# Three VectorE operations instead of six in a split of fp32 weights, and attention chunks that alternate between two batches

## The chip, the cores and the metric

The kernel runs on one core of a Trainium2 chip. The metric is the device time of one execution in microseconds; before the change it is 609.76 us, the median of three runs from 607.66 to 609.99.

## The reference

A decayed linear attention (2 batches, 8 heads, 768 positions, head size 64) feeds two feed-forward blocks in fp32 (512 to 2048 to 512 columns, 1536 tokens), the first with ELU, the second with softplus:

```python
for b in range(nb):                      # blocks of 64 positions
    intra = np.einsum('bhic,bhjc->bhij', qb, kb) * Dmask[None]
    intra = np.einsum('bhij,bhjd->bhid', intra, vb)
    inter = np.einsum('bhid,bhde->bhie', qb * lam_pow[None], kv_state)
    out[:, :, sl] = intra + inter
    kv_state = lam_block[None, :, None, None] * kv_state + np.einsum('bhsd,bhse->bhde', kb_dec, vb)
...
h = x @ w_in;  g = where(h > 0, h, exp(min(h, 0)) - 1);  x = g @ w_out
h = x @ w_in2; g = maximum(h, 0) + log1p(exp(-abs(h)));  y = g @ w_out2
```

## The kernel before

Attention works in chunks of 128 positions, six per batch, twelve in all, `g` counting through batch 0 and then batch 1. A chunk has three slots of TensorE work: "s" (`att_s`, scores, then masked by VectorE at L234), "t" (`att_state`, the new state from keys that ScalarE has scaled at L212, summed by VectorE at L281 and multiplied by the decay on POOL at L285, `faded`) and "x" (`att_x`, the output from scores and from the state of the chunk before, split into `xh` by ScalarE at L263 and `xl` by VectorE at L264). POOL multiplies the queries by decay powers at L206. The loads of later chunks (`qk`, `kv`) are issued in `att_next` from SP, after a chunk's "x".

The feed-forward weights come as float64, 16 blocks of 1 MB for each layer (`raw`), and `split_w` makes two fp32r parts of each: `wh`, and the remainder `wl`. It is a generator that is advanced piece by piece by `w_ops`. A piece is one VectorE operation, with what ScalarE does beside it; there are six: L99 and L101 assemble the low bits of the word, L106 and L109 rebuild the fp32 value in `t`, L112 keeps its exponent, L120 makes `wl`. ScalarE does L98 (a scaled copy of the high words) and L119 (`wh`). The last piece issues the load of the next block but one (`load_w`, L75); `raw` has two buffers.

Each product is three fp32r matmuls (`wh` with `xh`, `wh` with `xl`, `wl` with `xh`), 128 x 512 wide. There are 96 steps, 48 for each layer, two of them lagging: step n issues `m1(n)` (12 wide matmuls, L350 to L352), the activation, and `m2(n-2)` (12 wide matmuls, L415). Before step 0, 13 of attention's 36 slots are run, which completes the four chunks of the first token tile; steps 0 to 7 take three slots each. Steps 0 to 3 have 8 dummy matmuls each (`warm(4)` is traced as 8) and advance the split by 8 pieces, later steps by 4; eight splits are wanted by step 8, and from step 13 on `w_start` starts one every two steps, in three groups of eight, the second group's end and the third in layer 2 or shortly before it.

TensorE's and SP's orders are as written by hand throughout. Up to step 7 the orders of ScalarE, VectorE and POOL are set by a planner that goes by priorities (attention and the first activations stand above the splits); from step 8 on only VectorE's is. Every engine runs its own list in order.

Of the kernel before, what the change touches and what calls it, by code (L numbers as in the profile page):

```python
# [15 lines left out]
P = 128  # L16
# [20 lines left out]
def body(ctx, tc, lamc, ident, attqk, attkv, w1, w2, out):  # L37
# [31 lines left out]
    def load_w():  # L69
        if wnext[0] == len(wqueue):  # L70
            return
        layer, fc = key = wqueue[wnext[0]]
        wnext[0] += 1
        raw[key] = stage.tile([P, 2 * DM], U64, tag="raw", name="raw")
        nc.sync.dma_start(out=raw[key], in_=weights[layer][fc])  # L75
# [15 lines left out]
    def split_w(key):  # L91

        word = raw.pop(key).bitcast(U32).rearrange("p (n two) -> p n two", two=2)
        low, high = word[:, :, 0], word[:, :, 1]
        r = conv.tile([P, 2 * DM], F32, tag="r", name="r")
        ri = r.bitcast(U32)

        A.activation(out=r, in_=high.bitcast(F32), func=AF.Copy, scale=2.0 ** -112)  # L98
        V.tensor_scalar(out=high, in0=high, scalar1=23, scalar2=None, op0=ALU.logical_shift_left)  # L99
        yield  # L100
        V.scalar_tensor_tensor(  # L101
            out=high, in0=low, scalar=9, in1=high, op0=ALU.logical_shift_right, op1=ALU.bitwise_or)
        yield
        t = conv.tile([P, 2 * DM], F32, tag="t", name="t")
        ti = t.bitcast(U32)
        V.tensor_scalar(  # L106
            out=ti, in0=ri, scalar1=3, scalar2=0x7FFFF000, op0=ALU.logical_shift_left, op1=ALU.bitwise_and)
        yield
        V.scalar_tensor_tensor(  # L109
            out=ti, in0=ri, scalar=0x80000000, in1=ti, op0=ALU.bitwise_and, op1=ALU.bitwise_or)  # L110
        yield
        V.tensor_scalar(out=ri, in0=ti, scalar1=0xFF800000, scalar2=None, op0=ALU.bitwise_and)  # L112
        yield
        fc = key[0] * NF + key[1]
        k = fc % RING
        pool = wp if k < 8 else late["acc"]
        hi = pool.tile([P, 2 * DM], F32R, tag=f"wh{k}", name=f"wh{k}")
        lo = pool.tile([P, 2 * DM], F32R, tag=f"wl{k}", name=f"wl{k}")
        A.activation(out=hi, in_=t, func=AF.Copy)  # L119
        V.scalar_tensor_tensor(out=lo, in0=high, scalar=2.0 ** -43, in1=r, op0=ALU.mult, op1=ALU.mult)  # L120
        load_w()
        for i in range(2):
            o = slice(i * DM, i * DM + DM)
            wh[fc, i], wl[fc, i] = hi[:, o], lo[:, o]
# [76 lines left out]

    def att_prep(g):

        if g % CPB:
            q = at[g][0].rearrange("p (a i) -> p a i", a=NPAIR)
            G.tensor_tensor(out=q, in0=q, in1=qpow, op=ALU.mult)  # L206

    def att_prep_k(g):
        if g < NCHUNK and g % CPB < CPB - 1:
            for h in range(H):  # L210
                k = at[g][2][:, D * h:D * h + D]
                A.activation(out=k, in_=k, func=AF.Copy, scale=kdecay[:, h:h + 1])  # L212
# [26 lines left out]
    def att_x(g):  # L239
        a = at[g]  # L240
        ps = a_psum("xps")
        first = g % CPB == 0

        for p in range(0 if first else NPAIR):
            o = slice(P * p, P * p + P)
            for e in range(2):
                r = slice(64 * e, 64 * e + 64)
                T.matmul(ps[r, o], state[g - 1][r, p, :], a[0][r, o], start=(p == 0), stop=False, skip_group_check=True)  # L248
        for p in range(NPAIR):
            o = slice(P * p, P * p + P)  # L250
            for e in range(2):
                h = 2 * p + e
                T.matmul(  # L253
                    ps[64 * e:64 * e + 64, o], a[3][:, D * h:D * h + D], sc[g][:, e, p, :],
                    start=first, stop=True, skip_group_check=True,
                )
        t, c = divmod(g, TT // P)
        if c == 0:
            new_x(t)
        o = slice(c * P, c * P + P)  # L260
        ps = ps.rearrange("p (a i) -> p a i", a=NPAIR)
        hi, lo = xh[t][:, :, o], xl[t][:, :, o]
        A.activation(out=hi, in_=ps, func=AF.Copy)  # L263
        deferred.append(lambda: V.tensor_tensor(out=lo, in0=ps, in1=hi.bitcast(F32), op=ALU.subtract))  # L264

    def att_state(g):
        if g % CPB == CPB - 1:
            return
        a = at[g]
        ps = a_psum("stps")[:, :NPAIR * D]  # L270
        for p in range(NPAIR):
            for e in range(2):
                r = slice(D * e, D * e + D)
                o = slice(P * p + D * e, P * p + D * e + D)
                T.matmul(ps[r, D * p:D * p + D], a[2][:, o], a[3][:, o], start=True, stop=True, skip_group_check=True)
        ps = ps.rearrange("p (a i) -> p a i", a=NPAIR)
        state[g] = ap2.tile([P, NPAIR, D], F32, tag="state", name="state")
        if g % CPB == 0:
            V.tensor_copy(state[g], ps)
        else:  # L280
            V.tensor_tensor(out=state[g], in0=ps, in1=faded.pop(g - 1), op=ALU.add)  # L281
        if g % CPB < CPB - 2:
            faded[g] = ap2.tile([P, NPAIR, D], F32, tag="faded", name="faded")
            decay = qpow[:, :, P - 1:P].to_broadcast([P, NPAIR, D])
            G.tensor_tensor(out=faded[g], in0=state[g], in1=decay, op=ALU.mult)  # L285

# [116 lines left out]
    def m2(n):  # L403
        u, c = order[n]
        layer, t, begin, end = units[u]
        fc = layer * NF + c
        if c == begin:
            for m in range(KD):
                yps[m] = ps_y.tile([P, TT], F32, tag=f"y{m}", name=f"y{m}")
        g = gt.pop(n)  # L410
        for m in range(KD):
            s = slice(P * m, P * m + P)
            for i, (gi, wt) in enumerate(((0, wh[fc, 1]), (1, wh[fc, 1]), (0, wl[fc, 1]))):
                a, b = (wt[:, s], g[:, gi]) if layer == 0 else (g[:, gi, s], wt)
                T.matmul(yps[m], a, b, start=(c == begin and i == 0), stop=(c == end - 1 and i == 2))  # L415
        if c < end - 1:
            return
        summed = yacc.get((layer, t))
        if end < NF:
            if summed is None:  # L420
                yacc[layer, t] = new_acc(free.pop())
            for m in range(KD):
                if summed is None:
                    A.activation(out=yacc[layer, t][m], in_=yps[m], func=AF.Copy)
                else:
                    V.tensor_tensor(out=summed[m], in0=yps[m], in1=summed[m], op=ALU.add)
        elif layer == 0:
            new_x(t)
            for m in range(KD):
                if summed is None:  # L430
                    hi = xh[t][:, m, :]
                    A.activation(out=hi, in_=yps[m], func=AF.Copy)
                    V.tensor_tensor(out=xl[t][:, m, :], in0=yps[m], in1=hi.bitcast(F32), op=ALU.subtract)
                else:
                    y = summed[m]
                    V.tensor_tensor(out=y, in0=yps[m], in1=y, op=ALU.add)
                    split.append((t, y, m))
        else:
            if summed is None:
                o = xp.tile([P, KD, TT], F32, tag=f"xl{t}", name="o")  # L440
            for m in range(KD):
                r = t * TT + m * P
                if summed is None:
                    y = o[:, m, :]
                    A.activation(out=y, in_=yps[m], func=AF.Copy)
                else:
                    y = summed[m]
                    V.tensor_tensor(out=y, in0=yps[m], in1=y, op=ALU.add)
                nc.sync.dma_start(out=out[r:r + P, :], in_=y)
# [10 lines left out]

    def step(n):
        last = len(order) - 1
        pieces = 4 if n < 4 else 2

        early = n < LAG
        if early:
# [38 lines left out]
    with tc.manual_schedule(engines={ET.SP, ET.PE}):  # L505
        setup()
        decays()
        att_prep_k(0)
        while len(slots) > 3 * (NCHUNK - TT // P) - 1:
            refill()  # L510
            att_slot()
            w_ops(1, True)
        for n in range(8):
            step(n)
    with tc.manual_schedule(engines={ET.PE, ET.Activation, ET.Pool, ET.SP}):
# [7 lines left out]
def _layout(q, k, v, lam, win, wout, win2, wout2):  # L523
    def t(x):

        x = x.reshape(B, NPAIR, 2, CPB, P, D).transpose(0, 3, 2, 5, 1, 4)
        return x.reshape(NCHUNK, P, DM)

    def n(x):

        x = x.reshape(B, H, CPB, P, D).transpose(0, 2, 3, 1, 4)
        return x.reshape(NCHUNK, P, DM)

    def w(a, b):
# [30 lines left out]
```

## Time and profile before

| | |
|---|---|
| median of three runs | 609.76 us |
| lowest, highest | 607.66, 609.99 us |
| span of the profiled execution | 606.8 us |
| busy in the span: TensorE, its weight loads | 584.5, 480.0 us |
| busy: VectorE, ScalarE, POOL | 408.8, 340.7, 174.7 us |
| mean granted clock of TensorE | 0.994 of full |
| read from memory, written | 46.21, 3.15 MB |

The profile holds one execution; the page gives its span, first to last instruction, and no other time for it. Views used are the page (busy times, and the span in 40 slices of 15.2 us with busy shares in tenths), the busy times in chosen stretches, instructions grouped by source line, the list in order of time, the waits, and the chain of work that ended last.

### The profile page before, as it was taken

What the parts mean: (1) busy time and instruction counts of PE and PEld (TensorE: products, weight loads), DVE (VectorE), ACT (ScalarE), POOL (GpSimd) and SP (SyncE); (2) the same over time, 40 slices, a digit from 0 to 9 for tenths busy, and PEclk for the clock granted to TensorE, in tenths of its full rate; (3) what the DMA queues carried; (4) which work ended last, traced back from release to release, by engine and by line L of the source; (5) the groups of instructions that cost most, each with busy time, mean ns of one, the idle gap of its engine ahead of it and who ended that gap; (6) DMA issues with size and microseconds to landing.
All of it is one profiled execution on the core that took longest, in us unless ns stands there. A gap on an engine that the chain in (4) does not pass through costs nothing.

```text
span 606.8 us, 7845 instructions
## 1 busy us (share of the span) xinstructions
PE 584.5 (96%) x3058; PEld 480.0 (79%) x3058; DVE 408.8 (67%) x469; ACT 340.7 (56%) x577; POOL 174.7 (29%) x130
## 2 busy tenths in 40 slices
PE   7887899999999999999999999999999999999997
PEld 6775777888888888888888877887878888888885
DVE  6999973114578672216877996559999995565655
ACT  4756544244564553245555765757877775655552
POOL 1423223022122221253253363123223222222122
PEclk9999899999999999999999999999999999999999
DMA  8853652000322411001213111001213100100101
GB/s 321 343 210 139 252 187 82 1 0 1 119 91 69 139 69 71 0 1 63 77 70 139 69 70 69 1 0 64 77 70 138 70 1 2 69 1 1 70 1 69
DMA packets 10117, 49.86 MB, mean 82 GB/s; under 512 B 1248, under 2 KB 1376, under 8 KB 5984
## 3 DMA queue, kind: packets, MB, share of 16 engines
q1 hardware_dynamic: 10080, 49.36, 22.2%
q8 instruction: 24, 0.39, 0.2%
q14 instruction: 13, 0.11, 0.1%
HBM read 46.21 MB, written 3.15 MB: 81 GB/s over the span
## 4 chain that ended last, share of the span: by engine, by line
PE 80%; DVE 9%; issue 4%; ACT 3%; DMA 2%; POOL 2%; SPq 0%; DVEq 0%; ACTq 0%; POOLq 0%
PE y L415 38%; PE hps L351 13%; PE hps L350 13%; PE hps L352 13%; DMA qk<-attqk 1%; DVE t L109 1%; DVE raw L101 1%; DVE t L106 1%; PE xps L248 1%; PE xps L253 1%; DMA kv<-attkv 1%; PE sps L231 1%; DVE u L379 1%; POOL g L391 1%; DVE l L387 1%
## 5 line engine op out<-in xcount | busy, mean ns | idle before, releaser
L350 PE MATMUL hps<-xh,wh 128*128 128x512 f32 x384 | 151.1, 394 | 1.7 <-ACT xh L263 1.7
L351 PE MATMUL hps<-xl,wh 128*128 128x512 f32 x384 | 150.4, 392 | 2.2 <-DVE xl L264 2.2
L352 PE MATMUL hps<-xh,wl 128*128 128x512 f32 x384 | 150.0, 391 | 0.0
L415 PE MATMUL y<-wh,g 128*128 128x512 f32 x384 | 120.7, 392 | 3.3 <-POOL g L391 3.0
L391 POOL TENSOR_TENSOR g<-l,g 128x512 fp32r<-128x512 f32 x48 | 68.9, 1436 | 185.1 <-ACT g L390 159.6
L391 POOL TENSOR_TENSOR g<-v,g 128x512 fp32r<-128x512 f32 x48 | 65.7, 1368 | 187.0 <-ACT g L390 187.0
L415 PE MATMUL y<-g,wh 128*128 128x512 f32 x384 | 119.0, 391 | 0.0
L361 ACT ACTIVATE v<-hps 128x512 f32<-128x512 f32 x48 | 28.7, 597 | 122.9 <-PE hps L352 122.9
L385 DVE SCALAR_TENSOR_TENSOR v<-v,hps 128x512 f32<-128x512 f32 x48 | 32.8, 684 | 90.1 <-ACT v L362 89.8
L415 PEld LDWEIGHTS y<-wh,g 128*128 128x128 f32 x384 | 72.1, 188 | 21.9 <-POOL g L391 6.6
L351 PEld LDWEIGHTS hps<-xl,wh 128*128 128x128 f32 x384 | 72.5, 189 | 17.7 <-DVE xl L264 2.8
L350 PEld LDWEIGHTS hps<-xh,wh 128*128 128x128 f32 x384 | 72.5, 189 | 17.5 <-ACT xh L263 1.9
L352 PEld LDWEIGHTS hps<-xh,wl 128*128 128x128 f32 x384 | 72.5, 189 | 15.1
L415 PEld LDWEIGHTS y<-g,wh 128*128 128x128 f32 x384 | 71.6, 188 | 15.5 <-issue 0.2
L379 DVE SCALAR_TENSOR_TENSOR u<-u,e 128x512 f32<-128x512 f32 x48 | 44.0, 917 | 56.4 <-ACT l L373 56.4
L415 PE MATMUL y<-wl,g 128*128 128x512 f32 x192 | 74.8, 390 | 0.0
L415 PE MATMUL y<-g,wl 128*128 128x512 f32 x192 | 74.8, 389 | 0.0
L370 ACT ACTIVATE e<-hps 128x512 f32<-128x512 f32 x48 | 28.7, 597 | 68.9 <-PE hps L352 68.9
L387 DVE TENSOR_TENSOR l<-l,u 128x512 f32<-128x512 f32 x48 | 61.7, 1286 | 3.7
L120 DVE SCALAR_TENSOR_TENSOR wl<-raw,r 128x1024 fp32r<-128x1024 uint32 x32 | 46.5, 1453 | 1.0 <-DVE r L112 0.5
L119 ACT ACTIVATE wh<-t 128x1024 fp32r<-128x1024 f32 x32 | 33.8, 1056 | 22.1 <-DVE t L109 21.7
L415 PEld LDWEIGHTS y<-g,wl 128*128 128x128 f32 x192 | 36.0, 188 | 7.5
(58 smaller groups left out, 692.4 us busy)
## 6 DMA issues: line engine op xcount, KB each, us to landing
raw<-w SPq DMA_DIRECT2D x32, 1024.0 KB, 4.8
qk<-attqk SPq DMA_DIRECT2D x11, 512.0 KB, 5.8
kv<-attkv SPq DMA_DIRECT2D x10, 512.0 KB, 5.9
out<-yacc SPq DMA_DIRECT2D x8, 256.0 KB, 2.0
early<-attkv SPq DMA_DIRECT2D x2, 512.0 KB, 11.1
out<-o SPq DMA_DIRECT2D x4, 256.0 KB, 2.4
early<-attqk SPq DMA_DIRECT2D x1, 512.0 KB, 11.3
id_t<-ident SPq DMA_DIRECT2D x1, 64.0 KB, 2.0
```

Source lines behind the costliest of these rows:

```text
L119: A.activation(out=hi, in_=t, func=AF.Copy)
L120: V.scalar_tensor_tensor(out=lo, in0=high, scalar=2.0 ** -43, in1=r, op0=ALU.mult, op1=ALU.mult)
L350: T.matmul(ps, wh[fc, 0][:, o], h[:, k, :], start=(k == 0), stop=False)
L351: T.matmul(ps, wh[fc, 0][:, o], l[:, k, :], start=False, stop=False)
L352: T.matmul(ps, wl[fc, 0][:, o], h[:, k, :], start=False, stop=(k == KD - 1))
L361: A.activation(out=v, in_=ps, func=AF.Relu, scale=-1.0)
L370: A.activation(out=e, in_=ps, func=AF.Abs)
L379: V.scalar_tensor_tensor(out=u, in0=u, scalar=-1.0, in1=e, op0=ALU.add, op1=ALU.subtract)
L385: V.scalar_tensor_tensor(out=v, in0=v, scalar=-1.0, in1=ps, op0=ALU.add, op1=ALU.max)
L387: V.tensor_tensor(out=v, in0=v, in1=u[0], op=ALU.subtract)
L391: G.tensor_tensor(out=g[:, 1], in0=v, in1=g[:, 0].bitcast(F32), op=ALU.subtract)
L415: T.matmul(yps[m], a, b, start=(c == begin and i == 0), stop=(c == end - 1 and i == 2))
```

## The change

The split is remade. ScalarE now makes the fp32 bit pattern of the high word with Prelu, whose negative slope puts the sign where a shift by three brings it back, and a second operation turns the low word into the three missing bits with rounding (`c`, unsigned integers). VectorE shifts and masks, adds `c` as integers, and later subtracts `wh` to get `wl`. Three pieces replace six, so the numbers of pieces per call of `w_ops` are halved, and before step 0 only every second slot advances the split. `load_w` is called in the first piece. `t` has no buffer any more; `c` has one.

In attention, `g` now takes chunk 0 of both batches, then chunk 1 of both, and so on: the state used is that of `g - B` (B is 2), `state` and `faded` have three buffers, the inputs are laid out in that order, and the output rows are computed accordingly.

```diff
-        A.activation(out=r, in_=high.bitcast(F32), func=AF.Copy, scale=2.0 ** -112)
-        V.tensor_scalar(out=high, in0=high, scalar1=23, scalar2=None, op0=ALU.logical_shift_left)
+        A.activation(out=r, in_=high.bitcast(F32), func=AF.Prelu, scale=2.0 ** -112, alpha=-2.0 ** 32)
+        A.activation(out=c, in_=low, func=AF.Copy, scale=2.0 ** -29)
+        V.tensor_scalar(
+            out=ri, in0=ri, scalar1=3, scalar2=0xFFFFFFF8, op0=ALU.logical_shift_left, op1=ALU.bitwise_and)
+        load_w()
         yield
-        V.scalar_tensor_tensor(
-            out=high, in0=low, scalar=9, in1=high, op0=ALU.logical_shift_right, op1=ALU.bitwise_or)
-        yield
-        t = conv.tile([P, 2 * DM], F32, tag="t", name="t")
-        ti = t.bitcast(U32)
-        V.tensor_scalar(
-            out=ti, in0=ri, scalar1=3, scalar2=0x7FFFF000, op0=ALU.logical_shift_left, op1=ALU.bitwise_and)
-        yield
-        V.scalar_tensor_tensor(
-            out=ti, in0=ri, scalar=0x80000000, in1=ti, op0=ALU.bitwise_and, op1=ALU.bitwise_or)
-        yield
-        V.tensor_scalar(out=ri, in0=ti, scalar1=0xFF800000, scalar2=None, op0=ALU.bitwise_and)
+        V.tensor_tensor(out=ri, in0=ri, in1=c, op=ALU.add)
         yield
...
-        A.activation(out=hi, in_=t, func=AF.Copy)
-        V.scalar_tensor_tensor(out=lo, in0=high, scalar=2.0 ** -43, in1=r, op0=ALU.mult, op1=ALU.mult)
-        load_w()
+        A.activation(out=hi, in_=r, func=AF.Copy)
+        V.tensor_tensor(out=lo, in0=r, in1=hi.bitcast(F32), op=ALU.subtract)
...
-        first = g % CPB == 0
+        first = g < B
...
-                T.matmul(ps[r, o], state[g - 1][r, p, :], a[0][r, o], start=(p == 0), stop=False, skip_group_check=True)
+                T.matmul(ps[r, o], state[g - B][r, p, :], a[0][r, o], start=(p == 0), stop=False, skip_group_check=True)
...
-        state[g] = ap2.tile([P, NPAIR, D], F32, tag="state", name="state")
+        state[g] = ap3.tile([P, NPAIR, D], F32, tag="state", name="state")
...
-        pieces = 4 if n < 4 else 2
+        pieces = 2 if n < 4 else 1
...
-            w_ops(1, True)
+            if len(slots) % 2:
+                w_ops(1, True)
```

## Rows read from the trace of the kernel before

**Rows 1.** The page: busy time by engine, and two rows of the 40 slices.

```profile
PE 584.5 (96%) x3058; PEld 480.0 (79%) x3058; DVE 408.8 (67%) x469; ACT 340.7 (56%) x577; POOL 174.7 (29%) x130
...
PE   7887899999999999999999999999999999999997
...
DVE  6999973114578672216877996559999995565655
```

**Rows 2.** Stretches: length, busy us (instructions) by engine, clock, DMA share, GB/s.

```profile
6.00:32.00 26.00, 20.09 (x287) 16.96 (x284) 22.12 (x34) 17.47 (x49) 11.01 (x9) 1.00 0.86 341
32.00:77.00 45.00, 37.53 (x313) 30.73 (x311) 43.35 (x52) 25.24 (x50) 12.73 (x10) 0.92 0.57 210
...
338.00:369.00 31.00, 28.61 (x124) 22.82 (x122) 29.89 (x33) 22.63 (x36) 13.97 (x10) 1.00 0.23 86
418.00:491.00 73.00, 72.31 (x314) 58.17 (x312) 71.01 (x81) 55.41 (x83) 20.80 (x14) 1.00 0.24 87
```

**Rows 3.** VectorE's lines, 0 to 90 us: count, busy us, mean ns, idle before.

```profile
L101 DVE SCALAR_TENSOR_TENSOR raw<-raw 128x1024 uint32<-128x1024 uint32 x8 | 11.3, 1413 | 0.0
L120 DVE SCALAR_TENSOR_TENSOR wl<-raw,r 128x1024 fp32r<-128x1024 uint32 x8 | 11.3, 1412 | 0.1
L109 DVE SCALAR_TENSOR_TENSOR t<-r,t 128x1024 uint32<-128x1024 uint32 x8 | 9.7, 1217 | 0.1
L106 DVE TENSOR_SCALAR t<-r 128x1024 uint32<-128x1024 uint32 x8 | 7.8, 974 | 0.0
L112 DVE TENSOR_SCALAR r<-t 128x1024 uint32<-128x1024 uint32 x8 | 7.0, 870 | 0.1
...
L99 DVE TENSOR_SCALAR raw<-raw 128x1024 uint32<-128x1024 uint32 x8 | 6.0, 755 | 0.3 <-ACT r L98 0.3
```

**Rows 4.** The page's groups, whole span: a tensor_tensor with both inputs in SBUF.

```profile
L387 DVE TENSOR_TENSOR l<-l,u 128x512 f32<-128x512 f32 x48 | 61.7, 1286 | 3.7
```

**Rows 5.** VectorE in order of time: start us, us; two operations without POOL beside.

```profile
32.48 0.68 DVE L99 TENSOR_SCALAR raw<-raw 128x1024 uint32<-128x1024 uint32 x1
33.09 1.21 DVE L120 SCALAR_TENSOR_TENSOR wl<-raw,r 128x1024 fp32r<-128x1024 uint32 x1
```

**Rows 6.** ScalarE's lines, whole span.

```profile
L98 ACT ACTIVATE r<-raw 128x1024 f32<-128x1024 f32 x32 | 36.1, 1130 | 0.8 <-DMA raw<-w 0.8
...
L212 ACT ACTIVATE kv<-kv,kdecay 128x64 f32<-128x64 f32 x64 | 16.6, 336 | 9.5 <-DMA kv<-attkv 9.5
...
L140 ACT ACT_TABLE_LOAD x1 | 1.3, 1283 | 0.7 <-PEq L556 0.7
```

**Rows 7.** TensorE's waits, whole span: us in total, times, longest.

```profile
PE stps L275 <- ACT kv L212: 5.5, 5, 3.9
...
PE xps L248 <- POOL faded L285: 2.1, 1, 2.1
```

**Rows 8.** TensorE in order of time: start us, us, idle before and its releaser.

```profile
31.52 0.50 PE L351 MATMUL hps<-xl,wh 128*128 128x512 f32 x1 [1.34 <-DVE xl L264]
...
34.14 1.05 PE L137 MATMUL warm<-zero 128*128 128x128 f32 x8
...
77.00 0.50 PE L351 MATMUL hps<-xl,wh 128*128 128x512 f32 x1 [0.85 <-DVE xl L264]
```

**Rows 9.** The chain that ended last: start us, us; one step apart, then 29 apart.

```profile
89.34 1.09 PE sps L231 x16
...
98.84 1.09 PE sps L231 x16
...
333.19 2.72 PE y L415 x12
...
496.53 2.72 PE y L415 x12
```

**Rows 10.** SP's queue in order of time: start us and us of the issue, waits included.

```profile
21.34 0.33 SPq L75 DMA_DIRECT2D raw<-w  x1
...
40.98 9.49 SPq L75 DMA_DIRECT2D raw<-w  x2
```

More of the change, by code (lines that the diff above doesn't have):

```diff
@@ L95, in split_w @@
         r = conv.tile([P, 2 * DM], F32, tag="r", name="r")
+        c = acc.tile([P, 2 * DM], U32, tag="c", name="c")
         ri = r.bitcast(U32)
-        A.activation(out=r, in_=high.bitcast(F32), func=AF.Copy, scale=2.0 ** -112)
-        V.tensor_scalar(out=high, in0=high, scalar1=23, scalar2=None, op0=ALU.logical_shift_left)
-        yield
-        V.scalar_tensor_tensor(
-            out=high, in0=low, scalar=9, in1=high, op0=ALU.logical_shift_right, op1=ALU.bitwise_or)
-        yield
-        t = conv.tile([P, 2 * DM], F32, tag="t", name="t")
-        ti = t.bitcast(U32)
-        V.tensor_scalar(
-            out=ti, in0=ri, scalar1=3, scalar2=0x7FFFF000, op0=ALU.logical_shift_left, op1=ALU.bitwise_and)
-        yield
-        V.scalar_tensor_tensor(
-            out=ti, in0=ri, scalar=0x80000000, in1=ti, op0=ALU.bitwise_and, op1=ALU.bitwise_or)
-        yield
-        V.tensor_scalar(out=ri, in0=ti, scalar1=0xFF800000, scalar2=None, op0=ALU.bitwise_and)
+        A.activation(out=r, in_=high.bitcast(F32), func=AF.Prelu, scale=2.0 ** -112, alpha=-2.0 ** 32)
[3 more added lines that the diff above has]
+        load_w()
+        yield
+        V.tensor_tensor(out=ri, in0=ri, in1=c, op=ALU.add)
         yield
@@ L202, in att_prep @@
     def att_prep(g):
-        if g % CPB:
+        if g >= B:
             q = at[g][0].rearrange("p (a i) -> p a i", a=NPAIR)
@@ L208, in att_prep_k @@
     def att_prep_k(g):
-        if g < NCHUNK and g % CPB < CPB - 1:
+        if g < NCHUNK - B:
             for h in range(H):
@@ L266, in att_state @@
     def att_state(g):
-        if g % CPB == CPB - 1:
+        if g >= NCHUNK - B:
             return
@@ L276, in att_state @@
         ps = ps.rearrange("p (a i) -> p a i", a=NPAIR)
-        state[g] = ap2.tile([P, NPAIR, D], F32, tag="state", name="state")
-        if g % CPB == 0:
+        state[g] = ap3.tile([P, NPAIR, D], F32, tag="state", name="state")
+        if g < B:
             V.tensor_copy(state[g], ps)
         else:
-            V.tensor_tensor(out=state[g], in0=ps, in1=faded.pop(g - 1), op=ALU.add)
-        if g % CPB < CPB - 2:
-            faded[g] = ap2.tile([P, NPAIR, D], F32, tag="faded", name="faded")
+            V.tensor_tensor(out=state[g], in0=ps, in1=faded.pop(g - B), op=ALU.add)
+        if g < NCHUNK - 2 * B:
+            faded[g] = ap3.tile([P, NPAIR, D], F32, tag="faded", name="faded")
             decay = qpow[:, :, P - 1:P].to_broadcast([P, NPAIR, D])
@@ L441, in m2 @@
             for m in range(KD):
-                r = t * TT + m * P
+                i, b = divmod(t * (TT // P) + m, B)
+                r = b * S + i * P
                 if summed is None:
@@ L524, in t @@
     def t(x):
-        x = x.reshape(B, NPAIR, 2, CPB, P, D).transpose(0, 3, 2, 5, 1, 4)
+        x = x.reshape(B, NPAIR, 2, CPB, P, D).transpose(3, 0, 2, 5, 1, 4)
         return x.reshape(NCHUNK, P, DM)
     def n(x):
-        x = x.reshape(B, H, CPB, P, D).transpose(0, 2, 3, 1, 4)
+        x = x.reshape(B, H, CPB, P, D).transpose(2, 0, 3, 1, 4)
         return x.reshape(NCHUNK, P, DM)
```

## The prediction

> **What bounds the kernel now.** I read the page first: TensorE is busy for 96% of the span [rows 1], so only its idle time can be gained, some 22 us, and the rest of VectorE's 67% matters only where TensorE waits for it. The slices say where: TensorE is below nine tenths in the first five and in the last, and VectorE stands at nine in four of those five, and again in two stretches, slices 23 and 24 and 28 to 33 [rows 1]. The table by stretches makes it plain [rows 2]. From 32 to 77 us VectorE is busy 43.35 of 45.00 us, TensorE only 37.53, at a granted clock of 0.92 where it is otherwise 1.00 (the low level, 1.2 GHz, follows TensorE's longest pause, the 3.9 us of [rows 7]); ScalarE has 25.24. From 338 to 369 and from 418 to 491 us VectorE is busy 96 and 97%, and TensorE again has holes. Then I ask what VectorE does early: the lines of 0 to 90 us [rows 3] show the six operations of a weight split, eight times each: 11.3 + 11.3 + 9.7 + 7.8 + 7.0 + 6.0 = 53.1 us, 6.64 us a split. All else on VectorE there (masks, states, remainders of attention) fits in what is left. What TensorE waits for by name is mostly not VectorE [rows 7]: 5.5 us for keys scaled by ScalarE and 2.1 us for the query or state work of POOL; but ScalarE was waiting for kv loads, and SP, which issues them in order, stood behind weight loads that wait for the split's last VectorE operation: 9.49 us at one point [rows 10]. So VectorE bounds the stage both directly and through SP.
>
> **Part 1, the split.** Six VectorE operations become three: one one-input shift-and-mask, and two two-input ones (add, subtract). The shift-and-mask is L106's form and takes its early mean, 974 ns [rows 3]. No 1024-wide tensor_tensor is in the trace. Its nearest rows are the two-input 1024-wide operations: 1.21 us undisturbed [rows 5], 1.41 us as an early mean [rows 3]; and L387, the same operation at half the width, mean 1286 ns [rows 4], which doubled is 2.57 us (it runs beside POOL nearly always). I take 1.41, since it has the width and the stage; the ends are 1.21 and 2.57. A split then costs 0.97 + 2 x 1.41 = 3.79 us instead of 6.64: 2.85 us less, 8 x 2.85 = 22.8 us less of VectorE's work in the early stage (ends 8 x 3.2 = 26 and 8 x 0.5 = 4).
>
> ScalarE gets one more 1024-wide operation per split, on the strided low words. The nearest row is L98, the same strided read, 1130 ns [rows 6]; the low end is the same width without stride, not far below it, and the high end twice that, 2.26 us, because the operands are integers and no row shows ScalarE reading or writing them. I take 1.13. Prelu in place of Copy I cost at nothing (ends 0 and a table load, below). Five splits start in 32 to 77 us, so ScalarE has 25.24 + 5 x 1.13 = 30.9 us to do in what I expect to be some 38 us: 81%, no longer light.
> The Trainium skill (ScalarE: Activation LUTs, Rules for kernel authors) speaks against this move: multiplications and the like belong on VectorE, which is faster per element. The rows agree that it is: a one-input 1024-wide operation takes 0.68 us there [rows 5] and 1.13 us on ScalarE [rows 6]. By that rule c would sit on VectorE, 8 x 0.75 = 6 us more of its early work, and the forecast would come out about 3 us later; I go by the busy shares of the stretch instead, since VectorE is the full engine.
>
> The pieces are regrouped so that the pace stays: 13 + 4 x 8 = 45 pieces of six (7.5 splits) were issued by the end of step 3, now 7 + 4 x 4 = 23 of three (7.7). Nothing is gained or lost there.
>
> **Part 2, the weight load moved.** load_w went from the split's last piece to its first. On SP it now waits for ScalarE's c instead of VectorE's L120, two pieces earlier, so SP is not held for 9 us. But it also moves ahead of the attention loads: the third weight chunk, issued at 21.34 us [rows 10], now stands before chunk 4's qk and kv. In 6 to 32 us the DMA engines run at 0.86 of their time and 341 GB/s [rows 2]; 1.05 MB ahead of qk costs 3.1 us there, and the scores of chunk 4 stand before the last attention output that step 0 needs. Queued behind a waiting load_w on SP are the qk and kv loads; ScalarE and then TensorE wait for those.
>
> **Part 3, alternating batches.** Chunk g needs the state of g-2, not g-1. The chain through VectorE's state and POOL's faded gets twice the time; its visible price is 2.1 us, once [rows 7]. The counts of matmuls, scalings and POOL operations stay: ten states, ten scalings, eight faded. Another buffer for state and faded, and the output rows' new addresses, cost nothing: same sizes, same issues, hidden behind TensorE as now.
>
> **The sum, by stages.**
> A, to the first layer product. It begins in earnest at 31.52 us [rows 8], after a wait for xl behind VectorE's queue. VectorE sheds two splits' worth before that, 2 x 2.85 = 5.7 us, and the state wait of 2.1 us goes; the load order gives up to 3.1 us back. I take a gain of 4 us (ends 2 and 6).
> B, from there to the fifth layer product, 77.00 us [rows 8]: 45.5 us. TensorE's own need: one undisturbed step, with everything but the dummy matmuls, takes 98.84 - 89.34 = 9.50 us [rows 9]; the dummies are 1.05 us [rows 8], and the first two steps have no second product, 12 wide matmuls in 2.72 us [rows 9]. So 2 x (9.50 + 1.05 - 2.72) + 2 x (9.50 + 1.05) = 36.8 us. At most 8.7 us can be gained, the pause and the low clock behind it among them. With ScalarE at 81% and keys that come just in time I leave 1.7 us of waits: a gain of 7 us (ends 3 and 8.7).
> C, layer 2. From 333.19 to 496.53 us lie 29 steps [rows 9], 163.34 us, where 29 x 5.44 = 157.8 would do (5.44 is two blocks of 12 products of 2.72 us, the first of these rows being one): 5.6 us lost, while VectorE is full. Eight to ten splits fall there, each 2.85 us lighter, 23 to 28 us of VectorE; its 100.9 of 104 us comes down to some 75. ScalarE's pair r and c adds 1.13 us every second step to 22.63 of 31 [rows 2], to some 83%. I take 4 us (ends 2 and 5.3).
> D, elsewhere: TensorE is full from the sixth slice to the layer change [rows 1] and the end is untouched; zero.
> Together 4 + 7 + 4 = 15 us (ends 7 and 20). The profiled span is 606.8 us; the page gives no time around it, and the median of the runs, 609.76, is 3.0 above it (the lowest 0.9). So 606.8 - 15 + 3.0 = 594.8 us, ends 589.8 and 602.8.
>
> **Rivals.**
> 1. ScalarE and the loads take VectorE's place early. For it: 81% busy with in-order waits on loads, 1024-wide operations in front of the 0.34 us scalings [rows 6], and the weight load ahead of qk. Against it: ScalarE's split work has no due time before step 8 but for the first chunks. Then A gives 2, B 2 and C 3: 606.8 - 7 + 3.0 = 602.8 us.
> 2. The new operations are no lighter because they run beside POOL: the change halves the count and not the time. For it: L387's mean is twice a clear one [rows 4]. Against it: L101, L109 and L120 have two inputs too and average 1.22 to 1.41 [rows 3]. At 2.57 a split costs 6.1 us, 0.5 less; A and B give 2 together, C 1, state 1: 605.8 us.
> 3. No gain at all: what ScalarE now issues late costs what VectorE gives, 607 to 612 us.
> 4. Slower: Prelu isn't in the loaded table, and every split pays a load for it and one back. The single load there is takes 1283 ns [rows 6]; two per split are 2.57 us of ScalarE. In layer 1's body that hides; the 8 early and some 8 in layer 2 don't, 16 x 2.57 = 41 us, less ScalarE's slack there of about 6: 606.8 - 15 + 35 + 3 = 630 us. It decides from about 15 / 16 = 0.9 us per split, so even one load would. Against it: Relu, Abs, Copy, Exp and Ln all run on the one load of the trace.
> The Trainium skill (ScalarE: Activation LUTs, Table sets: the hidden batching unit) lists the simple functions as present in every set and doesn't name Prelu among them; by its price for a switch with the drain (What ACT_TABLE_LOAD costs), some 2.66 us, the load alone being as in the trace, the same 16 splits would cost 85 us.
>
> **How the numbers follow.** Forecast 0.67; rival 1 0.13; rival 2 0.08; rival 3 0.06; rival 4 0.06. The range runs from 588.5 us (all the upper ends, with the lowest run's 0.9 us around the span somewhat in view: 587.7 to 589.8) to 603.0, which takes in rival 1; rivals 2 to 4 make up the 0.2 left out. A half per cent, 3 us, is about what a measurement of this kernel can tell from no change: faster by that (under 606.7) 0.87, within 0.07, slower 0.06.
>
> **What would show it.** Right: three VectorE rows per split of 0.7 to 1.0, 1.2 to 1.5 and 1.2 to 1.5 us; VectorE's busy time down by some 90 us; the first layer product near 27.5 us and the fifth near 66; TensorE's clock at 1.00 throughout; steps of 5.44 us through most of 330 to 480. Wrong: two-input rows near 2 us (rival 2); ScalarE at nine tenths early, with TensorE waiting for scaled keys (rival 1); a second table load (rival 4); SP's wait for a weight load in front of a kv load that TensorE then waits for, which would break stage B.

## The result and the profile after

The changed kernel takes 601.11 us (median of four runs, 599.67 to 602.59) against 608.91 us before: a ratio of 0.987, with a 95% interval from 0.9842 to 0.9897. That is faster by 7.8 us, inside the range, and about half of the 15 us forecast. The span of its profiled execution is 597.9 us, 8.9 less than before. That execution was the fastest of the four (599.67 us), so the stages below add up to somewhat more than the medians differ.

The page of the changed kernel, with the rows that answer to [rows 1]:

```profile
PE 581.6 (97%) x3058; PEld 480.0 (80%) x3058; DVE 331.2 (55%) x373; ACT 370.4 (62%) x609; POOL 164.8 (28%) x130
...
PE   7799899999999999999999999999999999999997
...
DVE  6886532103355541214655786558788875565655
ACT  5879543334775663337666885668888775755552
```

VectorE no longer stands at nine in any slice, and lost 77.6 us of busy time; ScalarE gained 29.7 and is now the one that stands at nine, in the fourth slice. TensorE is below nine tenths in the first two slices, the fifth and the last; before, it was so in the first five and the last.

The same stretches as [rows 2] (length, busy us and instructions by engine, clock, DMA share, GB/s); the third is the last weight splits of layer 2, which come earlier by the time gained:

```profile
6.00:32.00 26.00, 19.55 (x262) 16.70 (x260) 20.21 (x30) 21.42 (x56) 7.87 (x7) 0.93 1.01 406
32.00:77.00 45.00, 41.75 (x384) 34.09 (x381) 29.37 (x38) 31.88 (x63) 16.24 (x13) 1.00 0.61 216
...
410.00:483.00 73.00, 72.36 (x320) 59.55 (x319) 59.71 (x61) 61.83 (x91) 16.96 (x13) 1.00 0.20 72
```

From 32 to 77 us VectorE fell from 43.35 to 29.37 us and the clock is 1.00 in this execution. From 6 to 32 us it is the other way: TensorE is busy a little less than before (19.55 us against 20.09), its clock is 0.93, and the DMA engines are busy all the time, at 406 GB/s where it was 341.

TensorE in order of time says what it stood for there:

```profile
25.01 1.93 PE L227 MATMUL sps<-qk 64*128 64x128 f32 x16 [2.96 <-DMA qk<-attqk]
...
33.43 0.50 PE L347 MATMUL hps<-xl,wh 128*128 128x512 f32 x1 [0.26 <-DVE xl L260]
...
72.35 0.50 PE L347 MATMUL hps<-xl,wh 128*128 128x512 f32 x1 [0.48 <-DVE xl L260]
```

The scores of chunk 4 wait 2.96 us for their qk; behind that pause matmuls run at the lower clock level, 1.2 GHz (granted clock 0.55 from 25 to 27 us; 1.93 us for a block of 16 that takes 1.16 else). The first layer product is under way at 33.43 us, 1.91 later than in [rows 8]; the fifth at 72.35, 4.65 earlier. So stage A lost 1.9 us, and stage B took 38.92 us instead of 45.48, 6.6 less. SP's queue shows why qk was late (start us, us of the issue with its wait):

```profile
6.58 6.40 SPq L75 DMA_DIRECT2D raw<-w  x2
13.07 0.38 SPq L179 DMA_DIRECT2D qk<-attqk  x1
```

The third weight block's issue waits at the head of the queue for ScalarE's c, and chunk 4's qk goes out behind it and lands behind its 1 MB; before, the block itself was issued at 21.34 us [rows 10].

In layer 2 the chain that ended last has these two rows 29 steps apart, as in [rows 9]:

```profile
328.88 2.72 PE y L411 x12
...
487.62 2.72 PE y L411 x12
```

158.74 us for 29 steps, against 163.34: 1.0 us over 29 x 5.44, where it was 5.6. Stage C gained 4.6 us. Together -1.9 + 6.6 + 4.6 = 9.3 of the 8.9 us in the span; the rest is small new waits behind the fifth product (0.8 us for masked scores in step 4).

The new operations, VectorE's from 0 to 90 us and ScalarE's and one more of VectorE over the whole span:

```profile
L109 DVE CUSTOM_DVE_ANT_0 r<-r,c 128x2048 uint16<-128x2048 uint16 x8 | 11.0, 1377 | 2.3 <-ACT c L103 2.3
L117 DVE TENSOR_TENSOR wl<-r,wh 128x1024 fp32r<-128x1024 f32 x8 | 10.6, 1322 | 4.1 <-ACT wh L116 4.0
L104 DVE TENSOR_SCALAR r<-r 128x1024 uint32<-128x1024 uint32 x8 | 6.8, 850 | 0.5 <-ACT r L102 0.3
...
L103 ACT ACTIVATE c<-raw 128x1024 uint32<-128x1024 uint32 x32 | 36.6, 1143 | 0.0
L102 ACT ACTIVATE r<-raw 128x1024 f32<-128x1024 f32 x32 | 36.1, 1129 | 0.0
...
L136 ACT ACT_TABLE_LOAD x1 | 1.3, 1283 | 0.7 <-PEq L554 0.7
...
L383 DVE TENSOR_TENSOR l<-l,u 128x512 f32<-128x512 f32 x48 | 76.4, 1592 | 4.7
```

The first line is the integer addition of `c`, which runs as a custom operation on half words. A split costs VectorE 1.38 + 1.32 + 0.85 = 3.55 us early, c costs ScalarE 1.14 us, and there is still one table load.

### The profile page after: what moved, and what is told of

It is laid out like the page before. It is cut to its first block, busy times and chain, and to the rows that moved or that the text cites. A ratio compares the mean times of both kernels' runs of the same rounds, so it can differ in the third digit from the quotient of the medians.

```text
span 597.9 us, 7791 instructions
## 1 busy us (share of the span) xinstructions
PE 581.6 (97%) x3058; PEld 480.0 (80%) x3058; DVE 331.2 (55%) x373; ACT 370.4 (62%) x609; POOL 164.8 (28%) x130
## 4 chain that ended last, share of the span: by engine, by line
PE 85%; ACT 5%; DVE 3%; DMA 3%; issue 2%; POOL 1%; SPq 0%; ACTq 0%; DVEq 0%; POOLq 0%
PE y L411 41%; PE hps L346 14%; PE hps L347 14%; PE hps L348 14%; DMA kv<-attkv 3%; PE xps L244 1%; PE xps L249 1%; DVE r L109 1%; ACT c L103 1%; PE sps L227 1%; ACT wh L116 1%; ACT kv L208 1%; DVE yacc L445 0%; DVE sc L230 0%; PE stps L271 0%
## 5 line engine op out<-in xcount | busy, mean ns | idle before, releaser
L411 PE MATMUL y<-wh,g 128*128 128x512 f32 x384 | 118.9, 390 | 0.8 <-POOL g L387 0.6
L387 POOL TENSOR_TENSOR g<-l,g 128x512 fp32r<-128x512 f32 x48 | 63.4, 1322 | 186.6 <-ACT g L386 173.5
L387 POOL TENSOR_TENSOR g<-v,g 128x512 fp32r<-128x512 f32 x48 | 62.9, 1310 | 188.1 <-ACT g L386 188.1
L383 DVE TENSOR_TENSOR l<-l,u 128x512 f32<-128x512 f32 x48 | 76.4, 1592 | 4.7
L375 DVE SCALAR_TENSOR_TENSOR u<-u,e 128x512 f32<-128x512 f32 x48 | 33.2, 692 | 71.5 <-ACT l L369 71.4
L117 DVE TENSOR_TENSOR wl<-r,wh 128x1024 fp32r<-128x1024 f32 x32 | 45.0, 1407 | 14.7 <-ACT wh L116 13.8
L109 DVE CUSTOM_DVE_ANT_0 r<-r,c 128x2048 uint16<-128x2048 uint16 x32 | 40.4, 1263 | 6.2 <-ACT c L103 4.5
```

The source lines that it names most:

```text
L109: V.tensor_tensor(out=ri, in0=ri, in1=c, op=ALU.add)
L117: V.tensor_tensor(out=lo, in0=r, in1=hi.bitcast(F32), op=ALU.subtract)
L375: V.scalar_tensor_tensor(out=u, in0=u, scalar=-1.0, in1=e, op0=ALU.add, op1=ALU.subtract)
L383: V.tensor_tensor(out=v, in0=v, in1=u[0], op=ALU.subtract)
L387: G.tensor_tensor(out=g[:, 1], in0=v, in1=g[:, 0].bitcast(F32), op=ALU.subtract)
```

## The experiments

Times are medians in us; "first" and "fifth" are the starts of the second matmul of the first and fifth layer product in the profiled execution, and B is the time between them (single executions, so these three are less sure than the medians). Ratios are to the kernel before in the same set of runs (608.3 to 609.7 us).

| kernel | time | ratio, 95% interval | span | first | fifth | B |
|---|---|---|---|---|---|---|
| before | 608.9 | | 606.8 | 31.52 | 77.00 | 45.5 |
| changed | 601.1 | 0.987 (0.9842 to 0.9897) | 597.9 | 33.43 | 72.35 | 38.9 |
| changed, again | 600.9 | 0.9866 (0.983 to 0.9902) | 599.5 | 34.01 | 73.61 | 39.6 |
| e1 load last | 597.8 | 0.9817 (0.9786 to 0.9848) | 596.3 | 29.96 | 70.14 | 40.2 |
| e2 split only | 599.6 | 0.9836 (0.9792 to 0.988) | 598.9 | 35.27 | 73.13 | 37.9 |
| e4 c twice | 605.9 | 0.9953 (0.9931 to 0.9975) | 606.0 | 35.99 | 76.95 | 41.0 |
| e5 c on VectorE | 602.9 | 0.9892 (0.9862 to 0.9923) | 601.3 | 35.81 | 76.99 | 41.2 |
| e6 split only, load last | 592.9 | 0.9748 (0.9726 to 0.9771) | 590.6 | 28.55 | 65.31 | 36.8 |
| e7 e1, keys on VectorE | 599.3 | 0.9861 (0.9834 to 0.9889) | 597.4 | 34.59 | 72.73 | 38.1 |
| e8 e1, second block later | 597.7 | 0.9823 (0.9796 to 0.9851) | 595.7 | 28.54 | 69.22 | 40.7 |
| e9 e6, chunk 5 scaled | 593.4 | 0.9744 (0.9715 to 0.9773) | 592.3 | 29.98 | 66.50 | 36.5 |
| e10 e6, chunk 5's state | 595.9 | 0.9802 (0.9763 to 0.9842) | 594.2 | 28.99 | 67.62 | 38.6 |
| e11 e1, even pace | 595.4 | 0.9783 (0.9758 to 0.9808) | 593.1 | 30.26 | 67.08 | 36.8 |
| e12 e6, even pace | 594.5 | 0.9764 (0.9734 to 0.9794) | 593.0 | 29.37 | 65.52 | 36.2 |

My theory after the result was that stage A had failed by the order of the loads on SP, the rival that ScalarE had become the bound of the first 75 us.

**e1, the load put back in the last piece.**

```diff
-        load_w()
         yield
         V.tensor_tensor(out=ri, in0=ri, in1=c, op=ALU.add)
...
         V.tensor_tensor(out=lo, in0=r, in1=hi.bitcast(F32), op=ALU.subtract)
+        load_w()
```

> The changed kernel with one edit: the weight load is issued again in the split's last piece, so that on SP the third weight block comes behind chunk 4's qk and kv as it did before the change. Theory 1 (the lost stage A is the order of the loads: chunk 4's qk, issued at 13.07 us behind a weight block that SP waited 6.40 us to issue, is landed only at 25.0 us): the scores of chunk 4 start at 22.5 us or earlier, the first layer product is under way near 29 us instead of 33.4, and the time is about 597 us (595 to 599). Theory 2 (ScalarE is the full engine before 33 us, 21.4 of 26 us, and the wait for qk only covers for it): the first product stays at 32 us or later and the time at 600 to 602 us.

The first product came 3.5 us earlier and the time fell 3.3 us, as theory 1 has it. TensorE of e1 in order of time:

```profile
22.16 1.16 PE L227 MATMUL sps<-qk 64*128 64x128 f32 x16
...
29.96 0.50 PE L347 MATMUL hps<-xl,wh 128*128 128x512 f32 x1 [0.48 <-DVE xl L260]
...
68.76 0.49 PE L346 MATMUL hps<-xh,wh 128*128 128x512 f32 x1 [1.97 <-ACT xh L259]
```

Chunk 4's scores start at 22.16 us without a wait. But the fifth product gained only 2.2 us of the 3.5: it stands 1.97 us for xh. ScalarE of e1 in order of time shows xh behind a split:

```profile
64.72 1.15 ACT L103 ACTIVATE c<-raw 128x1024 uint32<-128x1024 uint32 x1
67.17 1.06 ACT L115 ACTIVATE wh<-r 128x1024 fp32r<-128x1024 f32 x1 [1.29 <-DVE r L108]
68.13 0.58 ACT L259 ACTIVATE xh<-xps 128x512 fp32r<-128x512 f32 x1
```

ScalarE waits 1.29 us for VectorE's sum with `wh` at the head of its list, while the output that xh is made of has been there since 66.3 us.

The changed kernel was run once more beside e6 to e8:

> The changed kernel itself once more, beside the runs of this set, so that differences of 2 to 4 us are taken on one chip: 599 to 602 us.

It took 600.9 us, 0.2 from the first time. Its profile is of an execution at 601.28 us: the fifth product comes 1.3 us later than in the first profile, and the clock is 0.92 from 6 to 32 us and 0.93 from 32 to 77, where the first profile has 0.93 and 1.00. So a difference of a microsecond between two profiles, or of some hundredths of the clock, need not come from an edit.

**e2, the split alone**, attention batch after batch (the attention edits and the layout undone).

> The new split alone: attention's chunks run batch after batch as before, everything else as in the changed kernel. Theory 1 (the split brings nearly all; the alternation is worth the state waits, about 2 us): 601 to 604 us, with TensorE's wait for POOL's faded back at some 2 us. Rival (the alternation is what gave stage B its 6.6 us, since no output waits for the state of the chunk just before it): 606 us or more, with the fifth layer product 5 us later than the 72.35 us of the changed kernel.

599.6 us: not slower than the changed kernel. The split brings all of the gain; in this order of loads the first product comes 1.8 us earlier with the alternation, and B is 1.1 us longer. That 1.8 isn't the state wait that I had priced: TensorE waits 0.2 us for `faded` in e2, not 2 as theory 1 has it, and e2's profile has instead 1.7 us for scaled keys before the first product and a stretch at the lower clock (0.50 from 13 to 18 us). The times of the two can't be told apart (intervals 0.9792 to 0.988 and 0.9842 to 0.9897).

**e4, c issued twice.**

```diff
         A.activation(out=c, in_=low, func=AF.Copy, scale=2.0 ** -29)
+        A.activation(out=c, in_=low, func=AF.Copy, scale=2.0 ** -29)
```

> The changed kernel with the operation that makes c issued twice on ScalarE, 32 x 1.14 us more of its work and nothing else. Theory 1 (ScalarE has slack in every stage): 601 to 604 us, the fifth layer product at 73 to 75 us. Theory 2 (ScalarE took VectorE's place as the bound of the first 75 us): 8 x 1.14 = 9 us appear there, the fifth product at 79 to 82 us, and with the eight to ten splits of layer 2 the time is 610 us or more.

605.9 us, between the two. Of 9.1 us more on ScalarE early, 4.6 show at the fifth product, and in layer 2 its chain has some 3.7 us over 29 steps instead of 1.0. Its stretches from 6 to 32 and from 32 to 77 us:

```profile
6.00:32.00 26.00, 19.18 (x244) 16.59 (x242) 17.23 (x28) 21.25 (x51) 7.60 (x7) 0.87 0.93 372
32.00:77.00 45.00, 41.64 (x372) 33.94 (x371) 31.66 (x40) 40.06 (x75) 14.56 (x12) 0.92 0.58 211
```

ScalarE at 40.06 of 45 us has no room left. So it wasn't the bound at 31.88, but about half of what is added to it early costs time. A part of that half goes through SP, whose weight load waits for `c`: chunk 4's qk goes out at 14.14 us instead of 13.07, and 2.6 of the 4.6 us are there at the first product already.

**e5, c on VectorE.**

```diff
-        A.activation(out=c, in_=low, func=AF.Copy, scale=2.0 ** -29)
+        V.tensor_scalar(out=c, in0=low, scalar1=2.0 ** -29, scalar2=None, op0=ALU.mult)
```

> The changed kernel with c made by VectorE (a one-input multiplication on the strided low words, integers in and out) instead of ScalarE: four VectorE operations a split, two of ScalarE. If VectorE is still near its limit early, as the prediction had it, 8 x 0.75 to 0.95 us come back in the first 75 us and some in layer 2: 603 to 606 us. If VectorE now has room (29.4 of 45 us busy from 32 to 77 us) and ScalarE is the tighter engine: 599 to 601 us, no slower than the changed kernel.

602.9 us, between the two expectations; the fifth product comes at 76.99 us, 4.6 later, but layer 2 has no hole left. The Trainium skill (ScalarE: Activation LUTs, Rules for kernel authors) would have the multiplication on VectorE; here the operation is faster there (901 ns early against 1143) and the kernel isn't (602.9 us against 601.1, intervals that meet). Of the 4.6 us, 2.4 are there at the first product, behind a wait of 3.38 us for scaled keys.

**e6, the split alone with the load in the last piece** (e1 and e2 together).

> The new split alone, with the weight load in the split's last piece: the kernel of e1 with attention batch after batch as before. Theory 1 (the alternation pays once the loads no longer hold stage A): 599.5 to 601 us, the first layer product 1.5 to 3 us later than the 29.96 us of e1, behind a wait for POOL's faded. Rival (the alternation is worth nothing measurable in either order of loads): 597 to 599 us, as e1.

592.9 us. Neither expectation allowed for that: without the alternation the kernel is 4.9 us faster than e1, and the intervals don't meet. TensorE and the stretches of e6:

```profile
28.55 0.39 PE L347 MATMUL hps<-xl,wh 128*128 128x512 f32 x1
...
65.31 0.51 PE L347 MATMUL hps<-xl,wh 128*128 128x512 f32 x1 [0.48 <-DVE xl L260]
```

```profile
6.00:32.00 26.00, 22.19 (x300) 19.02 (x296) 20.83 (x33) 20.98 (x53) 12.33 (x9) 1.00 1.00 399
32.00:77.00 45.00, 43.23 (x392) 35.28 (x391) 30.52 (x39) 34.12 (x68) 13.09 (x12) 1.00 0.66 239
```

The clock is whole in both; the fifth product comes 4.8 us earlier than in e1, all that the time shows. Against e2 it says what the load order costs in batch order: 6.7 us, at the first product and in the time, where it is 3.3 in the alternating order (some 2 us of the 6.7 at the first product are e2's stretch at the lower clock, an estimate from three blocks of 16 matmuls that take 2.08, 1.97 and 1.34 us there and 1.16, 1.09 and 1.09 in e6). My theory of the alternation fell with it: TensorE waits 0.2 us for `faded` in e6 too, so it was the lighter split, and not the alternation, that took the 2.1 us of [rows 7] away. A new theory: in the alternating order the first ten chunks all make a state, where in batch order chunk 5 makes none. That moves a key scaling on ScalarE and a state on TensorE and VectorE from behind the fifth product to ahead of it. And chunk 6 reads a state in the alternating order, where in batch order chunk 1 does: a product with the state moves from ahead of the first layer product into B.

**e9 and e10, chunk 5's unread work added to e6**: first the scaling of its keys, then also its state (its multiplication by the decay left out). Nothing reads either.

```diff
-        if g < NCHUNK and g % CPB < CPB - 1:
+        if g < NCHUNK - 1:
...
-        if g % CPB == CPB - 1:
+        if g == NCHUNK - 1:
             return
...
-        if g % CPB == 0:
+        if g % CPB in (0, CPB - 1):
             V.tensor_copy(state[g], ps)
```

> The kernel of e6 (new split, batch after batch, load in the last piece) with one addition: ScalarE also scales the keys of chunk 5, 2.0 us in eight operations, which nothing reads. In the alternating order chunk 5 needs that scaling, in batch order it doesn't; so the alternation moves it ahead of the fifth layer product. Theory (ScalarE's list is tight there, and this is a good part of the 4.9 us that the alternation costs in e1 against e6): 594.5 to 596 us. Rival (the lists have room for it, the cost comes from elsewhere): 592.5 to 593.5 us.

> The kernel of e9 with the whole unread state of chunk 5: also its 16 matmuls on TensorE (0.47 us) and VectorE's copy (0.42 us); the multiplication by the decay on POOL is left out. This is the state work that the alternation pulls into the first steps, except for the 1.0 us of chunk 6's product with the state, which it has besides. Theory (what the alternation costs is state work done earlier): 595 to 597 us, most of the way from e6 to e1. Rival (it costs by where it puts operations in the planner's lists): 592.5 to 594 us.

The scaling alone costs nothing that can be told (593.4 us). With the state it is 595.9 us, 3.0 of the 4.9 us, at some 1.0 us of added TensorE and VectorE work (0.57 from start to start on TensorE, 0.42 on VectorE). TensorE's waits in e10 (us in total, times, longest), and ScalarE before the fifth product:

```profile
PE hps L347 <- DVE xl L260: 1.7, 2, 1.2
PE hps L346 <- ACT xh L259: 1.3, 1, 1.3
...
64.32 1.06 ACT L115 ACTIVATE wh<-r 128x1024 fp32r<-128x1024 f32 x1 [1.29 <-DVE r L108]
65.29 0.58 ACT L259 ACTIVATE xh<-xps 128x512 fp32r<-128x512 f32 x1
```

The 1.3 us for xh that e6 hasn't (0.2 there) and e1 has (2.0) are back, and with them a stretch at the lower clock (0.96 from 32 to 77 us, as in e1). So state work done earlier is the larger part. The lists shift with it: in e10 the fifth product's xh stands behind a split's `wh`, as in e1, where in e6 it stands before it (63.67 against 64.27 us). That this shift is why it costs more than its own length fits the rows and isn't shown by itself. The interval of e10 (0.9763 to 0.9842) overlaps that of e6 at its end, but all four of its runs (595.37 us and more) are above all four of e6 and of e9 (up to 594.07), so the sign is surer than the size; the last 1.9 us I didn't separate.

**e7, e1 with the keys scaled by VectorE.**

```diff
-            for h in range(H):
-                k = at[g][2][:, D * h:D * h + D]
-                A.activation(out=k, in_=k, func=AF.Copy, scale=kdecay[:, h:h + 1])
+            k = at[g][2].rearrange("p (h d) -> p h d", h=H)
+            V.tensor_tensor(out=k, in0=k, in1=kdecay.rearrange("p (h o) -> p h o", o=1).to_broadcast([P, H, D]), op=ALU.mult)
```

> The kernel of e1 with the scaling of attention's keys moved from ScalarE (eight 0.34 us operations a chunk, 2.0 us) to VectorE (one 512-wide operation of 0.7 to 1.3 us a chunk). Theory (after the load order, ScalarE's in-order list is what is left of the wait before the fifth product: 1.97 us for xh there, 1.1 us for scaled keys): TensorE's wait for scaled keys and for xh falls by 2 to 3 us, its clock stays at 1.00, and the time is 594 to 596 us. Rival (TensorE waits for the kv loads and the order of the lists, not for ScalarE's amount of work): within 1 us of e1, 597 to 599 us.

599.3 us: a miss. ScalarE falls to 28.16 of 45 us and B to 38.1, but the first product is late:

```profile
15.68 1.12 PE L270 MATMUL stps<-kv 128*64 128x64 f32 x16 [2.94 <-DVE kv L207]
```

The scaling now waits in VectorE's list, TensorE stands 2.94 us and its clock is 0.85 from 6 to 32 us. Less work on one engine was paid for by a place in another's list.

**e8, e1 with the second weight block's load behind chunk 4's loads.**

> The kernel of e1 with the second weight block's load also issued later, behind chunk 4's qk and kv. If the DMA engines still bound stage A (0.96 of their time from 6 to 32 us in e1): the first layer product comes 1 to 2.5 us earlier than 29.96 us and the time is 595.5 to 597 us. If stage A is now bound by the chain of attention itself, since in e1 no wait for chunk 4's qk is left: no change, 597 to 599 us, and a later split of block 1 could cost up to 1 us.

The first product came 1.4 us earlier, the fifth 0.9, the time not at all (597.7). So the loads still set stage A a little, and the gain isn't in the time; where it goes wasn't looked into.

**e11 and e12, one piece a call in steps 0 to 3**, for e1 and for e6.

```diff
-        pieces = 2 if n < 4 else 1
+        pieces = 1
```

> The kernel of e1 (alternating, load in the last piece) with one piece of the split per call in steps 0 to 3 as in the later ones, so that the eighth split is done at the end of step 7 instead of step 4. Theory (split operations stand in ScalarE's list in front of the remainder and the keys that the first five steps wait for): ScalarE is busy 28 to 31 of 45 us from 32 to 77 us instead of 34.5, the fifth product comes 2 to 3 us earlier than 70.14 us, 594.5 to 596 us. Rival (pace doesn't matter, the waits are for loads): 597 to 599 us. A third outcome: the fifth to eighth weight blocks come too late for step 8 and the time is above 600 us.

> The kernel of e6 with the even pace of e11. Its first five steps are within 1.7 us of what TensorE's own work there takes (37.0 against 35.3 us), so little is left: 591 to 593 us if the pace counts, 592.5 to 593.5 us if not; above 595 us if the later blocks come late.

On e1 it gives 2.4 us: the fifth product at 67.08 us, 3.1 earlier, ScalarE at 31.12 of 45 us, the wait for xh back to 0.2 us. That is the theory in place and, within 0.1 us each, in size. The intervals of the two overlap a little, but all four runs of e11 are below all four of e1. The even pace also spreads the weight loads (DMA share 0.49 from 32 to 77 us, where e1 has 0.64), and the two weren't separated. On e6, which hasn't that wait, it gains nothing by the fifth product (65.52) and costs a little later: TensorE 31.60 of 33 us from 77 to 110 us, where e6 has 33.00. The two times, 594.5 and 592.9 us, have intervals that meet.

e6 has the lowest median, and e9 can't be told from it: 592.9 us, by the ratios 1.2% less than the changed kernel and 2.5% less than the kernel before.

## Why the prediction was right, and where it wasn't

Range and sign held, and the mechanism did in B and C. The time is nearest to rival 1's 602.8 us, whose loads were one of the two causes of the shortfall, but its stages (gains of 2, 2 and 3 us) aren't what came (-1.9, 6.6 and 4.6): that the range holds the time rests on an upper end that was put there for rival 1, and is in part luck.

1. **The bound.** VectorE bounded the first 77 us and the two stretches of layer 2, as read from [rows 2]. With its work cut, B gave 6.6 us of 7 and C 4.6 of 4, and in e6, the split alone, the fifth product comes 11.7 us earlier than before.
2. **The split's price.** 3.55 us against 3.79 in the sum. The add, a tensor_tensor in the kernel, runs as a custom operation on 2048 half words; its early mean, 1.38 us, came out near the 1.41 of the row that I took by chance, since that row is another operation. Rival 2 falls. VectorE's lines add up to 90.6 us less (428.2 before, 337.6 now), as forecast; its busy time on the page fell by 77.6 only, since an operation that follows at once starts before the one ahead has ended (33.09 against 32.48 + 0.68 us in [rows 5]) and the page counts that overlap once: 19.4 us before, 6.4 now.
3. **c and Prelu.** 1143 and 1129 ns, as taken; one table load, so rival 4 falls.
4. **Stage A, the step that failed.** I forecast a gain of 4 us, with the load order taken off at "up to 3.1", and measured a loss of 1.9. The profiles take that apart: the split with the load in its old place and the old order of chunks (e6) gains 3.0 us, the alternation gives 1.4 of it back (e1), and the load order 3.5 (the changed kernel). The 1.4 is the least sure of these: e9's profile, in batch order, is as late at the first product as e1's. So the load's price was about right in this order, and the terms that were mis-sized are the relief, 5.7 + 2.1 us in the sum and 3.0 measured, and the alternation, at nothing. VectorE's relief was to come in whole, but what is late next was a load. My sign for this, SP's wait for a weight load ahead of an attention load, came true, for qk and in stage A, where I had looked for it in B.
5. **"The counts of matmuls, scalings and POOL operations stay"** was true and not enough. I priced the alternation at a state wait saved and nothing lost. The state wait went without it (0.2 us in e2 and e6). The work isn't more, but some of it is earlier, in the stage with no room: e6 against e1 puts it at 4.9 us when the loads are in place, and e10 shows 3.0 of these from chunk 5's state work alone. In the changed kernel's own order of loads no cost can be told (e2).
6. **TensorE's own need in B**, 36.8 us worked out from [rows 8, 9]: e11 reaches it, and in batch order, where the state of chunk 5 and chunk 6's product with one fall away, e12 is below it (36.2). My 1.7 us of waits on top became 2.1 in the changed kernel, 2.8 in its second profile.
7. **ScalarE.** 31.88 of 45 us; I had 81% of 38 us. It isn't the bound (e4, e9), but its list is near enough to full that what stands first in it costs time (e1, e11).
8. **What lies around the span.** The 3.0 us were the distance from one profiled execution to a median. In every run on record the time is 1.7 to 1.9 us above its span; with 1.8 the same sum gives 593.6 us, so this term isn't what failed.

The forecast of 594.8 us is about what the split alone is worth (e6): what the other two edits took back is the difference. What stays open is why e6 is ahead of e10 and e1 by more than the added work, beyond the xh wait and the clock that the traces show. The alternation in the kernel before, without the new split, wasn't tried.

## What to carry to other kernels

When a bound engine is relieved, work out stage by stage what is late next, and in a stage with a full DMA queue list the loads in order of when they are needed before moving one: a 1 MB block ahead of a 0.5 MB one cost 3.3 us here, and 6.7 in batch order. A reordering that keeps all counts still moves work between stages; count what has to be done before each deadline, not in total. Where several engines ran in-order lists near three quarters full, moving work between them was worth less than moving it out from in front of what was waited for (e7 against e11).

## What the runs showed of the hardware that I had not expected

A tensor_tensor with both inputs in SBUF that meets a POOL operation waits for it. VectorE and POOL of the changed kernel in order of time:

```profile
442.01 1.29 POOL L387 TENSOR_TENSOR g<-l,g 128x512 fp32r<-128x512 f32 x1 [4.78 <-ACT g L386]
442.19 1.66 DVE L383 TENSOR_TENSOR l<-l,u 128x512 f32<-128x512 f32 x1
443.88 0.69 DVE L384 SCALAR_TENSOR_TENSOR l<-hps,l 128x512 f32<-128x512 f32 x1
```

L383 starts 0.18 us into POOL's 1.29 us and takes 1.66 us, where the shortest of its 48 takes 0.68. The Trainium skill (SBUF — State Buffer, SBUF: two separate sides) calls the port pair that the two share an exclusive lock for a whole instruction; 1.29 - 0.18 of waiting and some 0.6 of work agree with that. The surprise is where the meetings fall. L387 of the kernel before and L383, the same operation, have means of 1286 [rows 4] and 1592 ns, and the operation just ahead of it went the other way:

```profile
L379 DVE SCALAR_TENSOR_TENSOR u<-u,e 128x512 f32<-128x512 f32 x48 | 44.0, 917 | 56.4 <-ACT l L373 56.4
...
L375 DVE SCALAR_TENSOR_TENSOR u<-u,e 128x512 f32<-128x512 f32 x48 | 33.2, 692 | 71.5 <-ACT l L369 71.4
```

Before, 29 of L387's 48 (not nearly all, as I had it) and 10 of L379's took over 1.55 us; now 44 of L383's and none of L375's do. Together the two cost 105.7 us before and 109.6 now: relieving VectorE moved the meetings from one operation to the next, and little more. That it is the earlier start of these operations that brings L383 to the moment when POOL starts is likely and wasn't tested.

ScalarE reads and writes 32-bit integers at the speed of fp32: 1143 ns for c against 1129 for r.
